# A conditioned transformer block on one core: first LayerNorm as (x - mean) * rs on GpSimd, and a new order for the first 260 tasks

## The chip, the cores and the metric

The kernel runs on one core of a Trainium2 chip. The metric is device time in microseconds (us). Engines carry their names from the profile: PE (matrix products; PEld is its weight load), ACT (scalar engine), DVE (vector engine), POOL (GpSimd), SP (which here only issues DMA transfers).

## What is computed

One block over 2048 tokens of width 512: a LayerNorm with scale and shift from a conditioning vector, linear attention over 32 heads of 16 with softmax features, a residual, a second LayerNorm of the same kind, and a gated feed-forward of width 1376. All inputs are bf16.

```python
mod = (_silu(c) @ w_mod).reshape(c.shape[0], 6, 1, -1)      # sa, ca, ga, sb, cb, gb
h = _layernorm(x, axis=-1) * (1 + ca) + sa
x = x + ga * _A_ref(h, A_wqkv, A_w_phi, A_wo)
h = _layernorm(x, axis=-1) * (1 + cb) + sb
x = x + gb * _B_ref(h, B_w_gate, B_w_up, B_w_down)
```

`_A_ref` makes q, k and v from h, multiplies q and k of each head by a 16 x 16 matrix `w_phi`, takes softmax of the result and of its negative as features, sums features times v over all tokens, and divides. The change touches only the first LayerNorm and the order of the work around it.

## The kernel before, in words

The 2048 tokens are 16 tiles of 128 rows. All work is cut into some 1,230 tasks, each a few instructions on one engine with the buffers it needs. A long string, `ORDER` (line 39), lists all tasks by hand. `arrange` (line 137) walks through it: it hands out buffers from small pools (eight PSUM banks, eight xn tiles, and so on, a freed one going to the end of its pool's line) and gives each task to an engine: the first in the task's list of alternatives, or the one that a letter behind `@` names (A is ACT, D is DVE, P is POOL). Each engine then runs its tasks strictly in this order and waits in front of each for what the task reads and for its buffer. So the string sets five queues at once: PE, ACT, DVE, POOL, and SP, which issues all large transfers.

The tasks that the change and the steps below it speak of (t is a tile, g a group of tiles: group 0 is tile 0, group 1 tile 1, group 2 tiles 2 and 3, and so on to group 8 with tiles 14 and 15; j is one of four 128-row blocks of the width):

- `ld_...` loads on SP: x in seven pieces (x0a, x0b, x1a, x1b, x2a, x2b, x3a), the k weights (wk0, wk1), four quarters of the first two vectors of w_mod (wm00a, wm00b, wm01a, wm01b), wv, the ga part of w_mod (wmga), the last three parts (wmm2), wo. `wqT0` to `wqT3` load the q weights transposed by DMA (line 669).
- `warm0`, `warm1_i` (line 600): idle products of 512 columns on PE, whose result nobody reads.
- `tpw`, `wTc` (lines 661, 664): transposes of the k weights on PE, and their copies out of PSUM. `fold1j`, `fold0j`, `foldc` (lines 679, 685): the k and q weights times the block-diagonal w_phi (`bd`, line 580, built on POOL), and their copies.
- `st1_t` (lines 702, 703): mean and variance of a tile on DVE. `rs1_g` (lines 709 and 710 on ACT, 712 and 713 on POOL): 1/sqrt(variance + eps). `nmr1_g` (line 718): -mean*rs for each tile of a group, on DVE. `xn1_t`: the normalized tile; tile 0 on DVE as (x - mean) * rs (line 729), tile 1 on ACT as x*rs + nmr (line 727), all others on POOL as x*rs + nmr (line 731).
- `tphgj` (line 744): transposes of the normalized group on PE; for groups 6 and 7 the DMA does it (`xT1_t`, line 736). `hm1_gj` (lines 751, 753): scale and shift by the conditioning, out of PSUM, on ACT or DVE (groups 6 and 7 also on POOL).
- `modc1.0`, `modc1.1` (line 630): the conditioning's products for the first LayerNorm, in two halves, out of columns of w_mod; `modc1c0`, `modc1c1` copy them. hm1 of blocks j = 0, 1 needs the first half, j = 2, 3 the second. `modca`, `modc2` (line 616): the rest of the conditioning.
- `Kt` (some in halves a and b, line 817), `Vt` (line 821), `Qt` (line 871): products of a tile with the folded k weights, the v weights, the folded q weights. `et`, `qet` (line 776): exponentials on ACT. `nt`, `qnt` (line 780): sums on DVE. `rt` (lines 794 and 795 on ACT, 798 on DVE): reciprocals. `phit`, `qphit`: features. `vat` (line 836): copy of v. `kvt` (line 282): features times v. `pTt` (line 874): transposes of q features by DMA.

What follows (attention output, second LayerNorm, feed-forward with tasks g, tg, u, hm, y) is the larger part of the string.

Of the kernel before, what the change touches and what calls it, by code (L numbers as in the profile page):

```python
# [51 lines left out]
phi6.0 hm1_73@P n9.0 r9.0@A kv5.0 gwa gra gwb e11.4 e14.0 K10 phi7.0@D kv6.0 K12 V10 kv7.0 e14.4 r8.0 n11.6 n11.2 r11.6 phi9.0 e10.0 e12.0 ld_wd ld_wu0 grb  # L52
n11.4 n14.0 r11.2 n14.4 r14.0 n10.0 r14.4@A phi8.0 va8 V11 V14 n12.0 e11.0 K13 n11.0 phi11.6 r11.4 wo1 r11.0 va10 r10.0@A va11 kv8.0 kv9.0 phi11.2@D phi11.0@D
phi10.0@D phi11.4@D V12 K15 e13.0 wmod_free ld_wg0 phi14.4 phi14.0 kv10.0 kv11.4 kv11.6 Q6 kv11.0 e13.4 r12.0@A e15.4 n13.0 n13.4 r13.0 r13.4 n15.4 e15.0 va14
V15 V13 qe6.0 va12 kv11.2 n15.0 r15.0 r15.4@A va13 phi13.4 Q5 phi15.4 phi13.0@D va15 phi15.0@D phi12.0@D wo0 wo3 Q3 kv12.0 kv13.0 kv14.0 kv15.0 qn6.0 kvn0 kvz0
kv13.4 kv14.4 kv15.4 kvz1 kvn1 num0a num1a num2a wo2 rd0a wo_all rd1a qe3.0 u0a num0b num4a num1b rd0b Q11 qe5.0 rd2a u0b u2a rd4a num2b qn3.0 u1a rd1b tpo0 Q8
qphi6.0@P qphi6.1@P oT0 out0 num4b rd2b u1b wd0 qe11.0 u2b qphi3.1@P qphi3.0@P x1_0 rd4b st2_0 qe8.0 Q7 qe7.0 tpo1 oT1 Q10 Q9 out1 Q15 oT2 rs2_0 qn5.0 nmr2_0
xn2_0 u4a u4b x1_1 qn7.0 tsw xnT0 out2 qphi5.1@P qphi5.0@P pT6 mod02 mod00 qphi7.0@P pT3 mod03@A mod01@A qe15.0 qphi7.1@P Q13 g0.8 x1_2 tg0.8 g0.1 st2_1 wd1
rs2_1 tg0.1 u0.8 u0.1 g0.0 num3b g0.4 hm0.1 hm0.8 pT5 qe9.0 tg0.4 g0.9 wd2 u0.4 u0.9 rd3b u3b tg0.9 g0.5 num3a hm0.4 hm0.9 u0.2 u0.0 num6a tg0.5 tg0.0 rd3a u3a
u0.5 g0.2 hm0.0 hm0.5 rd6a nmr2_1 qe10.0 tg0.2 oT4 g0.10 u0.10 wd6 hm0.2 g0.3 pT7 tg0.3 u6a g0.6 num6b u0.3 y0.0 y0.1 rd6b tg0.10 hm0.10 hm0.3 num5a num5b u6b  # L60
rd5b wd3 wd4 wd5 oT3 oT6 xn2_1 qe13.0 tg0.6 rd5a y0.2 u5b g0.7 tg0.7 out4 u5a oT5 qn11.0 u0.6 u0.7 xnT1 num7a hm0.6 hm0.7 mod13@A mod12@A rd7a x1_4 y0.3 out3
qphi11.1@P qphi11.0@P x1_3 st2_3 out6 mod10@A mod11@A g1.2 tg1.2 g1.1 tg1.1 num7b wd7 u1.3 u1.2 hm1.2 u7a g1.4 u1.1 y0.4 rd7b hm1.1 u1.4 y0.5 tg1.4 hm1.4 g1.0
g1.10 u1.10 g1.3 u7b st2_2 rs2_2 tg1.10 tg1.3 hm1.10 hm1.3 pT11 out5 tg1.0 u1.7 g1.7 x1_6 nmr2_2 u1.0 hm1.0 g1.5 u1.5 x1_5 qn10.0 wd8 y0.6 g1.6 oT7 xn2_2 xn2_3
g1.8 y0.7 Q14 y0.8 wd10 tg1.7 tg1.5 hm1.5 out7 u1.8 u1.6 st2_4 tg1.6 xnT2 xnT3 wd9 x1_7 qphi10.0 Q12 hm1.7 st2_6 mod21@P mod20@P qphi10.1@P y1.0 pT10 tg1.8
mod22@A mod23@A hm1.6 g1.9 y1.1 y1.2 tg1.9 u1.9 y0.9 y1.3 y1.4 g2.5 y0.10 g2.6 st2_5 qe12.0 st2_7 hm1.8 qn9.0 tg2.5 qe14.0 rs2_4 hm1.9 rs2_3 nmr2_4 y1.5 u2.0
g2.1 g2.0 tg2.0 xn2_7@D hm2.0 nmr2_3 fin0 y1.6 g2.2 tg2.2 u2.6 u2.2 hm2.2 u2.1 num11b y1.7 g2.4 rd11b u11b xn2_6@P xnT7 xnT6 u2.5 tg2.1 xn2_5 qphi9.1@P hm2.1
tg2.6 u2.8 xn2_4 hm2.5 g2.3 num11a rd11a u11a u2.9 qphi9.0@P xnT5 y1.8 xnT4 tg2.4 u2.4 hm2.4 hm2.6 tg2.3 g2.9 u2.3 hm2.3 g2.8 tg2.8 tg2.9 u2.7 mod41@P mod43@P
# [991 lines left out]
```

## Time and profile before

| what | value |
|---|---|
| median of 3 runs | 203.72 us (203.69 to 203.81) |
| the profiled execution | 205.47 us |
| its span in the profile | 203.7 us |
| PE busy | 197.0 us, 97% of the span |
| DVE busy | 160.6 us, 79% |
| ACT busy | 106.1 us, 52% |
| POOL busy | 102.8 us, 50% |
| mean granted PE clock | 0.992 |

The span is the time from the first to the last instruction that the profile shows; the execution's own time is 1.77 us longer. In rows of the time-ordered view the first number is the start, the second the time from start to end of the row (`x5` means five instructions merged into one row), and brackets give idle time of the engine before it and what ended it. Because instructions are pipelined, the price of one is better read from its start to the start of the next. Shares over the whole span say little here, since the first 70 us and the rest have different limits.

### The profile page before, as it was taken

The page shows a single profiled execution, that of the slowest core. Times are in us where ns is not written, and L with a number is a line of the kernel's source. Part 1 is how long each engine was busy: PE and PEld are TensorE (multiplying, and loading weights), DVE is VectorE, ACT ScalarE, POOL GpSimd, SP SyncE. Part 2 cuts the span into 40 slices and gives each one's busy share as a digit, 9 for nine tenths or more (in the row PEclk, how much of TensorE's full clock was granted, in tenths as well). Part 3 has the DMA queues.
Part 4 walks back from the last instruction along what each step waited for, and adds up shares of the span by engine and source line. Part 5 has one row for each costly group of instructions (what it writes and reads, how often), then busy time and mean ns, then how long its engine had stood idle before and what let it go on. Part 6 is the DMA issues. An engine that isn't in the chain of part 4 may idle for free.

```text
span 203.7 us, 4159 instructions
## 1 busy us (share of the span) xinstructions
PE 197.0 (97%) x1471; PEld 107.0 (53%) x1471; DVE 160.6 (79%) x375; ACT 106.1 (52%) x252; POOL 102.8 (50%) x144
## 2 busy tenths in 40 slices
...
GB/s 163 328 255 263 275 223 70 136 74 196 392 330 26 147 117 55 77 53 97 118 59 119 36 69 103 80 103 77 26 26 58 23 79 27 31 27 5 53 53 55
DMA packets 49453, 22.94 MB, mean 113 GB/s; under 512 B 38065, under 2 KB 47634, under 8 KB 49426
## 3 DMA queue, kind: packets, MB, share of 16 engines
...
HBM read 11.58 MB, written 2.10 MB: 67 GB/s over the span
## 4 chain that ended last, share of the span: by engine, by line
PE 79%; DMA 8%; ACT 5%; SPq 3%; DVE 3%; issue 1%
PE y_ps L485 19%; PE u_ps L447 18%; PE g_ps L447 17%; PE k_ps L817 6%; PE a_ps L356 6%; DMA wg_sb<-in_B_w_gate_dram 5%; PE v_ps L821 4%; DMA wmod_sb<-in_w_mod_dram 3%; PE q_ps L871 3%; ACT e L776 2%; PE num L326 2%; SPq L537 1%; PE g_ps L449 1%; PE tp_h L744 1%; PE kvacc L282 1%
## 5 line engine op out<-in xcount | busy, mean ns | idle before, releaser
L457 ACT ACTIVATE tg<-g_ps 128x512 bf16<-128x512 f32 (+5 forms) x66 | 28.8, 455 | 67.0 <-PE g_ps L447 39.4
L485 PE MATMUL y_ps<-wd_sb,wmod_sb 128*128 128x512 bf16 (+4 forms) x187 | 45.7, 366 | 0.0
L468 DVE SCALAR_TENSOR_TENSOR wmod_sb<-tg,u_ps 128x512 bf16<-128x512 bf16 (+4 forms) x63 | 30.2, 491 | 18.2 <-ACT tg L457 11.6
L447 PEld LDWEIGHTS <-wg_sb 128*128 128x128 bf16 (+1 forms) x252 | 21.9, 99 | 16.1
L447 PEld LDWEIGHTS <-wu_sb 128*128 128x128 bf16 (+1 forms) x252 | 21.9, 99 | 16.0 <-issue 0.3
L784 POOL TENSOR_TENSOR qphi<-qe,qks 128x512 bf16<-128x512 bf16 x24 | 25.1, 1060 | 3.9 <-DMA pT<-qphi 1.2
L485 PEld LDWEIGHTS <-wmod_sb 128*128 128x128 bf16 (+1 forms) x187 | 17.1, 98 | 16.0 <-issue 0.6
L447 PE MATMUL u_ps<-wT_sb,wu_sb 128*128 128x512 bf16 (+2 forms) x124 | 23.8, 322 | 0.0
L447 PE MATMUL g_ps<-wT_sb,wg_sb 128*128 128x512 bf16 (+2 forms) x124 | 23.1, 322 | 0.0
L447 PE MATMUL g_ps<-wqk_sb,wg_sb 128*128 128x128 bf16 (+4 forms) x128 | 20.0, 287 | 0.0
L447 PE MATMUL u_ps<-wqk_sb,wu_sb 128*128 128x128 bf16 (+4 forms) x128 | 19.8, 287 | 0.1
L780 DVE TENSOR_REDUCE ks<-e 128x64 f32<-128x1024 bf16 (+2 forms) x22 | 19.1, 904 | 0.4 <-ACT e L776 0.4
L780 DVE TENSOR_REDUCE qks<-qe 128x64 bf16<-128x1024 bf16 x16 | 19.2, 1204 | 0.0
L492 DVE TENSOR_TENSOR ot<-y_ps,x 128x512 bf16<-128x512 f32 (+2 forms) x17 | 11.0, 653 | 10.3 <-PE y_ps L485 10.2
L376 POOL TENSOR_SCALAR ve<-mv 128x2 f32<-128x2 f32 (+1 forms) x8 | 1.8, 221 | 33.8 <-DVE mv L366 33.7
L776 ACT ACTIVATE e<-k_ps 128x512 bf16<-128x512 f32 (+2 forms) x44 | 18.0, 515 | 0.0
L817 PE MATMUL k_ps<-wqk_f,h1T 128*128 128x512 bf16 x64 | 17.9, 402 | 0.0
L776 ACT ACTIVATE qe<-q_ps 128x512 bf16<-128x512 f32 x32 | 17.4, 618 | 0.6 <-POOL phi L787 0.4
L356 PE MATMUL a_ps<-wo_sb,oT 128*128 128x512 bf16 x64 | 16.3, 379 | 0.0
L787 POOL TENSOR_TENSOR phi<-e,kr 128x1024 bf16<-128x1024 bf16 (+2 forms) x10 | 14.4, 1449 | 3.6 <-ACT kr L795 2.1
L821 PE MATMUL v_ps<-wv_sb,h1T 128*128 128x512 bf16 x64 | 16.1, 379 | 0.0
L871 PE MATMUL q_ps<-wqk_f,h1T 128*128 128x512 bf16 x64 | 15.9, 379 | 0.0
...
## 6 DMA issues: line engine op xcount, KB each, us to landing
...
wu_sb<-in_B_w_up_dram SPq DMA_DIRECT2D x1, 1376.0 KB, 11.0
wg_sb<-in_B_w_gate_dram SPq DMA_DIRECT2D x1, 1376.0 KB, 10.4
...
```

What stands on the lines that cost most here:

```text
L356: pe.matmul(ap_[:], lhsT=oT[:, j, :], rhs=wo_sb[:, j, :], start=(j == 0), stop=(j == KT - 1))
L447: pe.matmul(ps[:fsz, 0:n], lhsT=w[:, j, ft * P:ft * P + fsz], rhs=h[:, j, 0:n], start=(j == 0), stop=(j == KT - 1))
L457: G.add(f"tg{k}.{ft}", {"ACT": 0.13 + n * 0.00083}, lambda e, tg=tg, g_ps=g_ps, fsz=fsz, n=n: act.activation(tg[:fsz, 0:n], g_ps[:fsz, 0:n ...
L468: dve.scalar_tensor_tensor(hm_all[:fsz, hm[k].slot, ft, 0:n], tg[:fsz, 0:n], 1.0, u_ps[:fsz, 0:n], op0=ALU.add, op1=ALU.mult)
L485: mm = pe.matmul(y[:, 0:c1 - c0], lhsT=hm_all[:fsz, hm[k].slot, ft, tl * P:(tl + 1) * P], rhs=wd_sb[:fsz, ft, c0:c1], start=(ft == 0), sto ...
L776: act.activation(ee[:, a:b, s].rearrange("p g f h -> p g (f h)"), kp[:, a * 64:b * 64].rearrange("p (g n) -> p g n", n=64), ACT.Exp, scale ...
L780: dve.tensor_reduce(ks[:, a:b].rearrange("p g s h -> p (g s) h"), ee[:, a:b].rearrange("p g s f h -> p (g s) h f"), axis=AX.X, op=ALU.add)
L784: engine(e).tensor_tensor(ph[:].rearrange("p (g s f h) -> p g s f h", s=2, f=DH, h=4)[:, :, s], ee[:, :, s], ks[:, :, 1 - s].unsqueeze(2). ...
L787: engine(e).tensor_tensor(ph[:, a * P:b * P].rearrange("p (g f h) -> p g f h", f=DH, h=4), ee[:, a:b].rearrange("p g s f h -> p (g s) f h" ...
L817: pe.matmul(kp[:], lhsT=h1T[:, j, t * P:(t + 1) * P], rhs=wqk_f[:, j, D:2 * D], start=(j == 0), stop=(j == KT - 1))
L821: pe.matmul(vp[:], lhsT=h1T[:, j, t * P:(t + 1) * P], rhs=wv_sb[:, j, :], start=(j == 0), stop=(j == KT - 1))
L871: pe.matmul(qp[:], lhsT=h1T[:, j, t * P:(t + 1) * P], rhs=wqk_f[:, j, 0:D], start=(j == 0), stop=(j == KT - 1))
```

## The change

Three things, and nothing else in the program:

1. xn1 of tiles 2 to 15 on POOL computes (x - mean) * rs, with the mean and rs as the two per-row operands, instead of x*rs + nmr. The nmr1 tasks of groups 2 to 8 are gone (seven tasks, 14 DVE instructions). Only tile 1, on ACT, keeps its one nmr1 product.
2. There are 14 idle products `warm1_i` instead of 12.
3. The first tasks of the string, all those ahead of `pT1`, stand in a new order: 274 before, 269 after. From `pT1 pT4 ld_wd2 tph81` on the string is unchanged, word for word. Some tasks change their engine: rs1_0 and rs1_6 from ACT to POOL, rs1_4 from POOL to ACT, wTc1 from ACT to DVE, r1.0 from DVE to ACT, hm1_00, hm1_42 and hm1_52 from DVE to ACT, hm1_13, hm1_20, hm1_41, hm1_43 and hm1_50 from ACT to DVE. In SP's queue wk1 goes ahead of wk0, x0b ahead of everything but x0a as before, wm00b ahead of x1a, wm01a ahead of wm01b; x3a and wv go ahead of wqT1, the four wqT stand in a row, wmga goes behind them and behind xT1_11 and xT1_10, and wo behind pT2.

The diff, with the string cut at the first lines of each version:

```diff
-wdz pmem warm0 ld_x0a st1_1 rs1_1 st1_0 c1 c2 ld_x0b warm1_0 warm1_1 warm1_2 warm1_3 ld_wk0 ld_wk1 nmr1_1 xn1_1@A st1_3 warm1_4 st1_2 rs1_0 xn1_0 tph11 tpw1
-tpw0 ld_x1b ld_x1a wTc1 warm1_5 tpw2 ld_wm00b c3 tph10 tph03 tph00 st1_7 tpw3 bd rs1_2@P tph13 wTc0 nmr1_2 xn1_3 xn1_2 warm1_6 ld_wm00a st1_6 wTc2 st1_4 st1_5
-wTc3 fold11 fold10 warm1_7 foldc11 ld_x2b fold13 warm1_8 st1_11 foldc10 fold12 warm1_9 foldc13 modc1.0 warm1_10 ld_wm01b tph20 foldc12 warm1_11 rs1_4@P nmr1_4
-ld_wm01a modc1c0 hm1_11@A hm1_10@A tph02 rs1_3@P tph01 tph23 hm1_20@A hm1_01@A st1_10 tph21 hm1_21@A hm1_00 modc1.1 modc1c1@D rs1_6 nmr1_3 tph22 tph12 ld_x2a
-wqT1 hm1_22 hm1_13@A hm1_03 xn1_7 K1a K0a hm1_02@A hm1_23@A xn1_6 tph42 tph40 xn1_5 hm1_40@A st1_8 tph41 ld_x3a xn1_4 K3a hm1_42 hm1_12@A ld_wv0 nmr1_6 tph43
-K3b hm1_41@A xn1_11 tph30 xn1_10 st1_9 rs1_5@P hm1_30@A tph31 wqT3 tph32 K1b ld_wmga st1_15 st1_14 hm1_31@A fold01 foldc01 K0b tph33 wqT2 rs1_8@P K2a K2b hm1_33
-nmr1_5 V0a wqT0 V0b V3a xn1_9 e3.0 V1a xT1_11 e0.0 fold03 n3.0 V1b nmr1_8 xn1_14 va0 e2.0 n0.0 st1_13 r0.0 modca.0 modca.1 xn1_15 st1_12 xn1_8 foldc03 n2.0
-modcac e1.0 hm1_32@A V2a fold02 phi0.0 n1.0 r1.0 fold00 V2b foldc02 foldc00 r3.0 va1 xT1_10 hm1_60@P ld_wmm2 va2 r2.0@A hm1_62@P tph82 hm1_82@A tph50 phi2.0@D
-phi1.0@D hm1_50@A hm1_63@P V3b K4a K4b rs1_7@P Q0 Q2 kv0.0 Q1 qe0.0 va3 qe2.0 hm1_43@A qe1.0 modc2.0 tph52 modc2.1 tph51 nmr1_7 xn1_12 xn1_13 phi3.0@D ld_wo
-qn0.0 modc2c e4.0 kv1.0 qn2.0 hm1_52 kv2.0 Q4 K5a kv3.0 xT1_12 xT1_13 qphi0.0@P qphi0.1@P qn1.0 qe4.0 qphi2.1 tph80 K5b hm1_80@A hm1_51@A e5.0 pT0 qphi2.0 n4.0
-r4.0@A qn4.0 n5.0 phi4.0@D qphi1.1@P hm1_61@P qphi1.0@P tph53 V5 K7a V4 va5 hm1_53@A V6 pT2 hm1_70@P qphi4.1 va4 hm1_71 mask4 va6 K6a K7b K6b e6.0 K8 tph83
-hm1_83 r5.0 qphi4.0@P e8.0 pT1 pT4 ld_wd2 tph81 hm1_81 n6.0 n8.0 e7.0 n7.0 V7 kv4.0 hm1_72@P K11 K9 V9 K14 V8 r6.0@A e9.0 va7 va9 r7.0@A e11.2 e11.6 phi5.0
...
+wdz pmem bd warm0 ld_x0a ld_x0b st1_1 c1 warm1_0 rs1_1 warm1_1 st1_0 rs1_0@P warm1_2 c2 nmr1_1 st1_2 st1_3 c3 xn1_1 warm1_3 warm1_4 warm1_5 warm1_6 ld_wk1 tpw2
+wTc2 rs1_2@P xn1_3 tpw3 xn1_2 xn1_0 tph10 ld_wk0 tpw1 tpw0 wTc3 wTc0 fold12 fold13 wTc1@D fold11 fold10 foldc12 foldc11 foldc10 warm1_7 warm1_8 tph20 warm1_9
+tph00 tph13 ld_x1b st1_6 st1_7 rs1_4 xn1_6 ld_wm00b ld_x1a st1_4 warm1_10 ld_wm00a xn1_7 st1_5 rs1_3@P xn1_4 foldc13 ld_x2b st1_11 modc1.0 tph01 warm1_11
+warm1_12 modc1c0 hm1_00@A hm1_10@A ld_wm01a tph23 tph21 tph11 hm1_20 tph40 tph22 warm1_13 tph41 hm1_21@A hm1_01@A hm1_40@A ld_wm01b st1_10 modc1.1 hm1_41 K3a
+hm1_11@A tph03 modc1c1@D hm1_13 hm1_23@A tph42 hm1_22 tph12 tph02 hm1_42@A hm1_12@A K0a K2a hm1_02@A xn1_5 hm1_03 ld_x2a st1_9 tph31 tph30 hm1_30@A hm1_31@A K3b
+tph32 hm1_32@A tph33 tph43 rs1_6@P xn1_11 xn1_10 st1_8 hm1_43 ld_x3a st1_14 st1_15 e3.0 K2b e2.0 hm1_33 ld_wv0 st1_13 rs1_5@P xn1_9 K0b e0.0 V1a V2a V1b rs1_8@P
+xn1_14 xn1_15 V3a V3b va3 K1a va1 wqT1 K1b fold01 V0a wqT3 wqT2 foldc01 fold02 e1.0 wqT0 fold03 n3.0 fold00 foldc00 V2b n0.0 n2.0 r0.0 xT1_11 foldc03 foldc02
+xT1_10 hm1_60@P hm1_63@P r2.0@A V0b V6 va0 n1.0 r1.0@A tph80 K4a K4b xn1_8 tph50 hm1_50 va2 ld_wmga modca.0 phi0.0 Q0 qe0.0 modca.1 modcac hm1_80@A st1_12
+rs1_7@P phi1.0@D Q1 qe1.0 kv0.0 phi2.0@D kv1.0 Q2 qe2.0 kv2.0 K6a tph53 hm1_53@A hm1_62@P r3.0 phi3.0@D Q4 e4.0 qe4.0 V5 va5 xn1_13 ld_wmm2 xT1_13 K5a kv3.0
+xn1_12 xT1_12 qn0.0 qphi0.0@P qphi0.1@P pT0 qn1.0 K5b K6b qn2.0 qphi2.0 qphi2.1 pT2 n4.0 tph51 e5.0 n5.0 tph52 hm1_52@A modc2.0 modc2.1 va6 r4.0@A hm1_51@A K7a
+tph82 hm1_82@A V4 va4 modc2c qn4.0 phi4.0@D K7b qphi1.0@P hm1_61@P qphi1.1@P hm1_71 e6.0 K8 qphi4.1 tph83 mask4 hm1_83 r5.0 hm1_70@P qphi4.0@P e8.0 ld_wo pT1
+pT4 ld_wd2 tph81 hm1_81 n6.0 n8.0 e7.0 n7.0 V7 kv4.0 hm1_72@P K11 K9 V9 K14 V8 r6.0@A e9.0 va7 va9 r7.0@A e11.2 e11.6 phi5.0 phi6.0 hm1_73@P n9.0 r9.0@A kv5.0
...
@@ -600,7 +599,7 @@
                 pe.matmul(ps[:], lhsT=wd_sb[:, FT - 1, 0:P], rhs=wd_sb[:, FT - 1, :], start=True, stop=True)
         G.add(nm, {"PE": dur}, f, bufs=[ps], **kw)
     warm("warm0", 6, 2.4, r=["wdz"], w=["warm"])
-    for i in range(12):
+    for i in range(14):
         warm(f"warm1_{i}", 1, 0.22, r=["c1"], w=["warm"])
 
     def modc_task(nm, chs, rks, wk, f2, dur):
@@ -712,7 +711,7 @@
                 pool.tensor_scalar(ve1[:, sl], mv1[:, sl, 1], 1e-5, None, op0=ALU.add)
                 pool.tensor_tensor(rs1[:, sl], ve1[:, sl], mhalf[:, sl], op=ALU.pow)
         G.add(f"rs1_{g}", {"ACT": 0.43, "POOL": 1.1}, f_rs, r=[("mv1", t) for t in ts], w=[("rs1", g)])
-        if g:
+        if g == 1:
             def f_nm(e, ts=ts):
                 for t in ts:
                     dve.tensor_scalar(nmr[:, 0, t:t + 1], mv1[:, t, 0:1], rs1[:, t:t + 1], -1.0, op0=ALU.mult, op1=ALU.mult)
@@ -725,11 +724,9 @@
             def f_xn(e, t=t, xn=xn):
                 if e == "ACT":
                     act.activation(xn[:], x_sb[:, t, :], ACT.Identity, scale=rs1[:, t:t + 1], bias=nmr[:, 0, t:t + 1])
-                elif e == "DVE":
-                    dve.tensor_scalar(xn[:], x_sb[:, t, :], mv1[:, t, 0:1], rs1[:, t:t + 1], op0=ALU.subtract, op1=ALU.mult)
                 else:
-                    pool.tensor_scalar(xn[:], x_sb[:, t, :], rs1[:, t:t + 1], nmr[:, 0, t:t + 1], op0=ALU.mult, op1=ALU.add)
-            G.add(f"xn1_{t}", {"POOL": 0.69, "ACT": 0.73} if t else {"DVE": 0.3}, f_xn, r=[("rs1", g)] + ([("nmr1", g)] if t else []), w=[("xn1", t)],
+                    engine(e).tensor_scalar(xn[:], x_sb[:, t, :], mv1[:, t, 0:1], rs1[:, t:t + 1], op0=ALU.subtract, op1=ALU.mult)
+            G.add(f"xn1_{t}", {"ACT": 0.73} if t == 1 else {"POOL": 0.69} if t else {"DVE": 0.3}, f_xn, r=[("rs1", g)] + ([("nmr1", g)] if t == 1 else []), w=[("xn1", t)],
                   bufs=[xn], port=("POOL", "DVE"))
         if TD[g]:
             for q, t in enumerate(ts):
```

More of the change, by code (lines that the diff above doesn't have):

```diff
@@ L52 @@
[L52 to L67, printed above, removed]
```

53 lines of the change are left out of this document (34 added, 19 removed).

## The prediction

> **What bounds the kernel now.** I read the page first for the span, then busy time by stretches, then each engine in order of time over the first 45 us, then the waits there, and last the transfers. The profiled execution took 205.47 us: the span and 1.77 us around it. The median without profile is 203.72 us, 1.75 us less, so I work out a difference on the trace and take it from the median.
>
> ```profile
> span 203.7 us, 4159 instructions
> ```
> ```profile
> 4.02:7.43 3.41, 2.32 (x20) 1.08 (x19) 3.27 (x11) 2.08 (x7) 1.71 (x3) 1.00 1.04 325
> 10.85:14.26 3.41, 2.92 (x48) 1.85 (x47) 3.23 (x14) 3.12 (x11) 3.24 (x7) 1.00 1.26 218
> 14.26:17.67 3.41, 3.41 (x16) 1.76 (x15) 3.13 (x10) 2.54 (x7) 2.60 (x5) 0.50 1.15 345
> 11.80:40.87 29.07, 28.50 (x267) 16.25 (x267) 27.35 (x60) 27.59 (x66) 24.20 (x34) 0.94 0.87 197
> 13.44:40.25 26.81, 26.62 (x255) 15.22 (x253) 25.16 (x53) 25.33 (x61) 22.02 (x29) 0.94 0.84 203
> 41.00:58.00 17.00, 17.00 (x138) 8.72 (x136) 16.86 (x34) 16.58 (x54) 13.63 (x11) 1.00 0.87 245
> 70.00:200.10 130.10, 129.97 (x875) 70.30 (x873) 95.69 (x225) 44.35 (x97) 45.97 (x64) 1.00 0.33 64
> ```
>
> The columns behind the stretch's length are PE, PEld, DVE, ACT, POOL, granted clock, DMA share, GB/s. From 70 us to the end PE never rests, and from 41 to 58 us PE, DVE and ACT are all full. So the part of the order that the change leaves alone runs as one solid block, and what decides is how early the new first part hands over to it. I set the fourth and fifth stretch so that they end with that part's last task on ACT (e8, 40.87 us) and on DVE (r5, 40.25 us); on PE the part ends with V7. All three engines must come earlier if the block is to come earlier: the smallest of the three shifts is the gain.
>
> In 11.80 to 40.87 us ACT is idle for 29.07 - 27.59 = 1.48 us, and in 13.44 to 40.25 us DVE for 1.65 us. Most of that has one cause:
>
> ```profile
> ACT h1T L751 <- PE tp_h L744: 1.3, 2, 0.7
> DVE h1T L753 <- PE tp_h L744: 0.9, 2, 0.6
> ```
>
> Both wait for PE's transposes, at 15 to 20 us, and PE is late there because its clock is granted at 0.50 for just one stretch, 14.26 to 17.67 us: 3.41 us at half speed lose 1.71 us of products. Why does the clock fall there? PE in the stretch two before it (kept its clock) and in the one just before the fall:
>
> ```profile
> 4.11 1.25 PE L600 MATMUL warm<-wd_sb 128*128 128x512 bf16 x5
> 6.41 0.23 PE L744 MATMUL tp_h<-ident,xn 128*128 128x128 bf16 x1 [1.05 <-POOL bd L580]
> 6.68 0.62 PE L661 MATMUL tp_w<-ident,wqk_sb 128*128 128x128 bf16 x8
> 7.13 0.38 PE L600 MATMUL warm<-wd_sb 128*128 128x512 bf16 x1
> ```
> ```profile
> 11.36 0.38 PE L600 MATMUL warm<-wd_sb 128*128 128x512 bf16 x1
> 11.79 0.27 PE L744 MATMUL tp_h<-ident,xn 128*128 128x128 bf16 x2
> 11.90 0.38 PE L600 MATMUL warm<-wd_sb 128*128 128x512 bf16 x1
> 12.34 0.60 PE L744 MATMUL tp_h<-ident,xn 128*128 128x128 bf16 x6
> 13.26 0.55 PE L630 MATMUL modc_ps<-sc_bf,wmod_sb 128*128 128x1 bf16 x16 [0.32 <-DMA wmod_sb<-in_w_mod_dram]
> 13.67 0.47 PE L744 MATMUL tp_h<-ident,xn 128*128 128x128 bf16 x3
> 13.98 0.77 PE L817 MATMUL k_ps<-wqk_f,h1T 128*128 128x512 bf16 x2
> ```
>
> Busy time does not explain it: 2.92 us before the fall, only 2.32 us where the clock stayed. Columns streamed do: 5 x 512 + 128 + 8 x 128 + 512 = 4224 where it stayed; 2 x 512 + 11 x 128 + at most 2 x 512 = 3456 before the fall (the modc products stream one column each). So I take it that somewhere between 3456 and 4224 columns in 3.41 us the clock is kept.
>
> **The change, part by part.** *PE and its clock.* The start stays where it is: modc1.1 waits for the last quarter of w_mod, which is as before behind ten earlier loads of the same sizes, so it starts near 13.26 us (the row with the DMA wait). Ahead of it the new order puts three idle products (warm1_11 to 13) and twelve transposes into the deciding stretch, and behind it K3a and three transposes by 14.26 us: 3 x 512 + 12 x 128 + 2 x 512 + 3 x 128 = 4480 columns, above the 4224 that kept the clock. I forecast that the half-clock stretch goes. The two added products themselves stand ahead of modc1.1 or in the wait for the first weights; they cost nothing while PE has to wait for that load anyway, and at about 0.22 us each (five took 1.25 us with their tail) 0.44 us if that cover is gone. Behind modc1.1, PE's work to V7 is the old one less about four transposes (0.2 us). PE's term: 1.71 + 0.2 = 1.9 us.
>
> The Trainium skill, "TensorE: Matmul & The Clock Gate", Part 1, says that a free-running window of about 3.4 us sets the clock and that it falls after an idle window. The length agrees with 3.41 us; the idle window does not, for PE was busy 2.92 us of the one before the fall.
>
> *ACT.* Rows of its prices, each to the start of the next:
>
> ```profile
> 11.80 2.07 ACT L751 ACTIVATE h1T<-tp_h,modc 128x128 bf16<-128x128 bf16 x5
> 13.74 0.31 ACT L709 ACTIVATE ve<-mv,eps 128x2 f32<-128x2 f32 x1
> 14.08 0.20 ACT L710 ACTIVATE rs<-ve 128x2 f32<-128x2 f32 x1
> 14.19 1.24 ACT L751 ACTIVATE h1T<-tp_h,modc 128x128 bf16<-128x128 bf16 x3
> ```
> ```profile
> 24.34 0.68 ACT L751 ACTIVATE h1T<-tp_h,modc 128x256 bf16<-128x256 bf16 x1
> 24.79 1.20 ACT L685 CAST wqk_f<-fold_ps 128x512 bf16<-128x512 f32 x2
> ```
> ```profile
> 26.68 0.43 ACT L794 ACTIVATE ks<-ks 128x64 f32<-128x64 f32 x1
> 27.21 0.26 ACT L795 ACTIVATE kr<-ks 128x64 bf16<-128x64 f32 x1
> 27.37 1.00 ACT L751 ACTIVATE h1T<-tp_h,modc 128x256 bf16<-128x256 bf16 x2
> ```
>
> An hm1 of one tile is 1.94/5 = 0.39 us, of two 0.45, an rs1 0.45, an r 0.69. Behind 11.80 us ACT loses hm1_20, 41, 43, 50 (1.80), hm1_13 (0.39) and rs1_6 (0.45) and gains hm1_00 (0.39), hm1_42, 52 (0.90) and r1.0 (0.69): 0.66 us less. With PE on time its 1.33 us of waiting goes, and 0.15 us stays: 11.80 + 27.59 - 0.66 + 0.15 = 38.88 against 40.87. ACT's term: 2.0 us. I looked where ACT could wait anew: the fold copies, e, va and qe each find their product finished earlier when PE runs at full clock, so none is late next.
>
> *DVE.*
>
> ```profile
> 21.78 0.33 DVE L718 TENSOR_SCALAR nmr<-mv,rs 128x1 f32<-128x1 f32 x2
> 22.02 1.21 DVE L780 TENSOR_REDUCE ks<-e 128x64 f32<-128x1024 bf16 x1
> ```
> ```profile
> L753 DVE TENSOR_SCALAR h1T<-tp_h,modc 128x256 bf16<-128x256 bf16 (+1 forms) x8 | 2.9, 375 | 0.9 <-PE tp_h L744 0.9
> L798 DVE RECIPROCAL kr<-ks 128x64 bf16<-128x64 f32 x4 | 2.0, 528 | 0.0
> ```
>
> A pair of -mean*rs costs 0.24 us; seven pairs go, five of them behind 13.44 us: 1.20. Five hm1 come and three go (2 x 0.375 = +0.75), r1.0 goes (-0.53): 0.98 us less. Its 0.9 us of waits for transposes goes, 0.75 stays: 13.44 + 25.16 - 0.98 + 0.75 = 38.37 against 40.25. DVE's term: 1.9 us. wTc1 on DVE has no row; a half-size read from PSUM is the 0.375, so 0.4 to 0.75 us, and it stands ahead of DVE's wait for the next rows of x, which hides it; without that cover it costs ACT's next fold copy as much.
>
> *POOL.* (x - mean) * rs has the same shape as the old form; no row shows it on POOL, so I bound it by the shortest and the longest of the old ones,
>
> ```profile
> L731 POOL TENSOR_SCALAR xn<-x_sb,rs,nmr x14: 762/767/1182, 9.5 to 31.2; 128x512 bf16<-128x512 bf16 x14
> ```
>
> 0.76 and 1.18 us, and take the median, 0.77; one subtraction in place of an addition gives no reason for less. POOL no longer waits for DVE's products, takes rs1_0 and rs1_6 and gives up rs1_4 (about 1 us more in all). On a walk with these prices the sixth xn1 is ready near 14.7 us and its transposes are due near 15.4; at 1.18 us each that cover is gone and about 1 us of the gain with it.
>
> *SP.* The first transposed load of the q weights (wqT1) moves behind x3 and wv, so that all four now stand in a row; w_mod's ga part moves behind the last two of them and two transposes of xn1 (so it now waits for POOL's xn1_11 and xn1_10), wo behind pT2, and pT1 now queues behind wo. Users: the q folds, due near 21 us; modca, due near 24 us; wo, due after 50 us. I cost these at nothing; the rival below is that this fails.
>
> **Sum.** PE 1.9, ACT 2.0, DVE 1.9: the block starts 1.9 us earlier, and everything behind it with it. 205.47 - 1.9 = 203.57 profiled, **201.8 us** for the median of 203.72. With DVE's remaining idle gone and PE's short stops too, at most 2.4; with xn1 at its dear end, 1.0.
>
> **Rivals.** *The clock doesn't change.* Either 4480 columns don't hold it, or the stretch's edges lie elsewhere against the work, or the runs without a profile never had the fall (the 1.75 us by which they are shorter is close to the 1.71 us). In the first cases PE stays the bound and gains its 0.2 us and its few short stops (28.50 us busy of 29.07); in the last ACT has 0.66 us less to do and DVE 0.98. All give about 0.7 us, 0.2 to 1.1: 203.0. For it: thin margin in columns. Against it: the three runs lie within 0.12 us, which a wandering fall would spread. By the skill's idle window the two idle products would not matter, since no window was idle, which is this rival.
>
> *Slower: the q weights come late.*
>
> ```profile
> 10.89 0.57 SPq L537 DMA_DIRECT2D x_sb<-in_A_x_dram  x1
> 11.52 0.50 SPq L551 DMA_DIRECT2D wv_sb<-in_A_wqkv_dram  x1
> 12.06 1.62 SPq L669 DMA_TRANSPOSE wT_sb<-in_A_wqkv_dram  x1
> ```
> ```profile
> x_sb<-in_A_x_dram SPq DMA_DIRECT2D x1, 512.0 KB, 5.1
> ```
> ```profile
> wT_sb<-in_A_wqkv_dram SPq DMA_TRANSPOSE x1, 7.4
> ```
>
> x3 lands at 10.89 + 5.1 = 16.0 us, the transposed load behind it and wv at 12.06 + 7.4 = 19.5: of these 3.5 us wv's 512 KB take about 1.6, so one transposed load may take 1.9. Four in a row behind wv (near 17.1 us) end at 24.7 at that price. PE reaches fold00 near 21.4 us (13.7 + 14 half K and V of two products, 6.2, + 27 transposes and folds at 0.45/8, 1.5), and V2b, V0b, V6, K4, Q0 queue behind it: 3.3 us of waiting against 1.9 gained, 205.1 us. It decides from a landing near 23.7 us on. Against it: SP issues x3, wv and the four in a row from about 9.3 us (10.89 less one transposed load of 1.6), so the fourth is issued near 9.3 + 0.57 + 0.50 + 3 x 1.62 = 15.2 us, and even at the 7.4 us that include a queue of 1 MB it lands at 22.6.
>
> *The gain is given back* between 41 and 70 us by something tied to a fixed time: no load there is, all hang on SP's order, so little chance; 203.7.
>
> **Numbers.** Less than 0.2% (0.41 us) a measurement of this kernel can't tell from no change. Forecast 0.50 (201.4 to 202.7), clock rival 0.27 (202.6 to 203.5, 0.03 of it within 0.2%), given back 0.09, slower 0.14. Faster 0.74, same 0.12, slower 0.14. The range goes from 2.4 us gained to 0.2, 201.3 to 203.5, and leaves out the slower rival and part of the same.
>
> **What would show it.** Granted clock 1.00 from 14 to 18 us; V7 on PE 1.9 us earlier, e8's end on ACT near 38.9, r5's on DVE near 38.4; no wait of ACT or DVE for tp_h over 0.3 us; no PE wait at the q folds. Wrong if the 0.50 stretch stands, if it appears at another place with PE due, or if V7 comes early and 70 us does not.

## The result and the profile after

The changed kernel takes 223.03 us (median, 222.92 to 223.61) against 203.76 us for the kernel before: 1.094 times as long, 95% interval 1.089 to 1.098. The prediction of 201.8 us was wrong, and its sign too.

The first view is the changed kernel's page: the span, then the chain that ended last, by engine and by line.

```profile
span 221.9 us, 4119 instructions
...
PE 59%; POOL 17%; DVE 9%; ACT 5%; DMA 4%; issue 3%; SPq 0%; POOLq 0%; ACTq 0%; DVEq 0%
PE y_ps L484 17%; PE u_ps L446 16%; PE g_ps L446 16%; POOL xn L728 12%; PE a_ps L355 5%; ACT e L773 3%; DMA pT<-qphi 3%; DVE ks L777 2%; PE num L325 2%; POOL rs L712 2%; DVE st L701 1%; DMA x_sb<-in_A_x_dram 1%; PE g_ps L448 1%; PE q_ps L868 1%; POOL qphi L781 1%
```

One line of POOL now carries 12% of the chain, 27 us. It is the changed normalization (line 731 before, 728 now). Its own view gives shortest, median and longest in ns, and who waited for it:

```profile
L728 POOL TENSOR_SCALAR xn<-x_sb,mv,rs x14: 2069/2074/2087, 8.6 to 45.7; 128x512 bf16<-128x512 bf16 x14
...
  PEld L741: 13.3, 6
  PE tp_h L741: 10.4, 6
```

One instruction takes 2.07 us where it took 0.77. The longest is within 1% of the shortest, which speaks against contention with a neighbour; the forms below settle it. The transposes wait for it, and what waits for the transposes follows. The stretches (the columns are those of the prediction) and the first stop on PE, in order of time:

```profile
10.00:20.00 10.00, 6.34 (x60) 4.14 (x62) 5.11 (x16) 4.74 (x14) 9.81 (x8) 0.59 0.86 222
20.00:30.00 10.00, 9.70 (x60) 4.71 (x58) 8.19 (x16) 8.65 (x19) 9.63 (x8) 0.89 0.16 27
30.00:40.00 10.00, 3.54 (x19) 1.38 (x19) 2.10 (x4) 2.53 (x8) 9.81 (x9) 0.62 0.56 210
```
```profile
9.13 0.59 PE L599 MATMUL warm<-wd_sb 128*128 128x512 bf16 x2
12.76 0.39 PE L741 MATMUL tp_h<-ident,xn 128*128 128x128 bf16 x2 [3.04 <-POOL xn L728]
...
18.02 0.61 PE L629 MATMUL modc_ps<-sc_bf,wmod_sb 128*128 128x1 bf16 x16
```

From 10 to 40 us POOL is the only engine that is full in all three stretches (9.81, 9.63, 9.81 of 10); PE is full in the second alone (9.70). modc1.1, forecast near 13.26 us, comes at 18.02, since PE takes its tasks in order and the transposes of the second pair stand ahead of it. The clock falls on top: 0.59, 0.89 and 0.62 in these stretches. It falls for the first time within the 3.04 us stop, near 11.9 us, when PE has been idle for 2.2 us. The Trainium skill ("TensorE: Matmul & The Clock Gate", Part 1) says that the clock falls after an idle window of some 3.4 us; the trace does not agree, for PE was busy for 1.25 of the 3.41 us ahead of the fall. What the lower clock adds to the loss is not told apart here; around 35 us it can't be much, since PE has work for 3.54 us of ten.

V7 shows how late the unchanged block begins (the prediction let the reordered part end with it; in the string it is the second task on PE behind that part). In order of time, the changed kernel:

```profile
56.28 1.03 PE L818 MATMUL v_ps<-wv_sb,h1T 128*128 128x512 bf16 x4
```

In the profile of before it stood at 39.13 us (its row is shown further down), 17.15 us earlier; the two profiled executions differ by 223.61 - 205.47 = 18.1 us. The last microsecond comes at the very end, and is taken up below.

### The profile page after: what moved, and what is told of

It is laid out like the page before. It is cut to its first block, busy times and chain, and to the rows that moved or that the text cites. A ratio compares the mean times of both kernels' runs of the same rounds, so it can differ in the third digit from the quotient of the medians.

```text
span 221.9 us, 4119 instructions
## 1 busy us (share of the span) xinstructions
PE 201.9 (91%) x1450; PEld 109.0 (49%) x1473; DVE 161.2 (73%) x363; ACT 105.9 (48%) x249; POOL 122.9 (55%) x146
## 4 chain that ended last, share of the span: by engine, by line
PE 59%; POOL 17%; DVE 9%; ACT 5%; DMA 4%; issue 3%; SPq 0%; POOLq 0%; ACTq 0%; DVEq 0%
PE y_ps L484 17%; PE u_ps L446 16%; PE g_ps L446 16%; POOL xn L728 12%; PE a_ps L355 5%; ACT e L773 3%; DMA pT<-qphi 3%; DVE ks L777 2%; PE num L325 2%; POOL rs L712 2%; DVE st L701 1%; DMA x_sb<-in_A_x_dram 1%; PE g_ps L448 1%; PE q_ps L868 1%; POOL qphi L781 1%
## 5 line engine op out<-in xcount | busy, mean ns | idle before, releaser
L484 PE MATMUL y_ps<-wd_sb,wmod_sb 128*128 128x512 bf16 (+4 forms) x180 | 44.2, 366 | 0.2
L467 DVE SCALAR_TENSOR_TENSOR wmod_sb<-tg,u_ps 128x512 bf16<-128x512 bf16 (+4 forms) x63 | 30.2, 491 | 18.1 <-ACT tg L456 11.6
L728 POOL TENSOR_SCALAR xn<-x_sb,mv,rs 128x512 bf16<-128x512 bf16 x14 | 29.0, 2076 | 0.5
L814 PE MATMUL k_ps<-wqk_f,h1T 128*128 128x512 bf16 x61 | 19.4, 440 | 1.4 <-ACT e L773 1.3
L868 PE MATMUL q_ps<-wqk_f,h1T 128*128 128x512 bf16 x61 | 17.4, 406 | 0.2
L741 PE MATMUL tp_h<-ident,xn 128*128 128x128 bf16 x48 | 7.4, 271 | 10.7 <-POOL xn L728 10.4
```

Of the source, the lines that this page charges most:

```text
L467: dve.scalar_tensor_tensor(hm_all[:fsz, hm[k].slot, ft, 0:n], tg[:fsz, 0:n], 1.0, u_ps[:fsz, 0:n], op0=ALU.add, op1=ALU.mult)
L484: mm = pe.matmul(y[:, 0:c1 - c0], lhsT=hm_all[:fsz, hm[k].slot, ft, tl * P:(tl + 1) * P], rhs=wd_sb[:fsz, ft, c0:c1], start=(ft == 0), sto ...
L728: engine(e).tensor_scalar(xn[:], x_sb[:, t, :], mv1[:, t, 0:1], rs1[:, t:t + 1], op0=ALU.subtract, op1=ALU.mult)
L814: pe.matmul(kp[:], lhsT=h1T[:, j, t * P:(t + 1) * P], rhs=wqk_f[:, j, D:2 * D], start=(j == 0), stop=(j == KT - 1))
L868: pe.matmul(qp[:], lhsT=h1T[:, j, t * P:(t + 1) * P], rhs=wqk_f[:, j, 0:D], start=(j == 0), stop=(j == KT - 1))
```

## The experiments

The theory after the result: the form on POOL is the whole loss (14 x 1.3 us, all on the path), and order and idle products do what the prediction said. The rival: the new order loses by itself, whatever a normalization costs. Both turned out to be partly right. Times are medians; the kernel before, timed again beside each group of runs, stood at 203.8 to 204.0 us.

### One part of the change alone

**order_only**: the new order and the 14 idle products, with the old x*rs + nmr and the nmr1 tasks put back by hand ahead of their users, for which six xn1 tasks and one rs1 stand at other places in the string. Tile 1's normalization falls to POOL in it; **order_old_form** puts it back on ACT.

```diff
-                    engine(e).tensor_scalar(xn[:], x_sb[:, t, :], mv1[:, t, 0:1], rs1[:, t:t + 1], op0=ALU.subtract, op1=ALU.mult)
+                    pool.tensor_scalar(xn[:], x_sb[:, t, :], rs1[:, t:t + 1], nmr[:, 0, t:t + 1], op0=ALU.mult, op1=ALU.add)
```

> The new order with its two more idle products, but xn1 on POOL again as x*rs + nmr, with the seven nmr1 tasks put back where DVE passes when rs1 is ready. Theory A (the form is slow: 14 instructions of 2.07 us in place of 0.77): POOL's xn1 rows return to 0.77 us, PE's waits for POOL xn (10.4 us after the change) shrink below 1 us, and the time is near or below the kernel before, 201.8 to 203.8 us. Theory B (the order is at fault: late q weights, POOL's tasks queued badly, and the long xn1 rows only show contention with DVE): the time stays above 214 us.

> The run order_only again with one slip mended: tile 1's xn1 had fallen to POOL there, ahead of everything, and is back on ACT. New order, x*rs + nmr on POOL, nmr1 tasks put in by hand. Theory A1 (with the form at 0.77 us the order is worth what the prediction said): 201.8 to 203.5 us. Theory A2 (the order is worth nothing once POOL and DVE hand -mean*rs back and forth again): POOL waits for nmr about 3 us as in order_only (3.2 us) and the time is 204 to 206 us.

Measured: 208.12 us (ratio 1.019, 1.015 to 1.023) and 206.53 us (1.013, 1.012 to 1.015), both above every range expected for theory A. So the new order with the old form costs 2.7 us; it does not gain. This is not yet the order alone: POOL waits 3.2 us for the products that were put back (nmr), between 4 and 60 us of order_old_form.

**form_only**: the old order and 12 idle products, with (x - mean)*rs on POOL and the nmr1 tasks of groups 2 to 8 gone.

> The old order and 12 idle products, but xn1 of tiles 2 to 15 on POOL as (x - mean) * rs, without the seven nmr1 tasks. Theory A: xn1 rows at 2.07 us, 14 x 1.30 = 18.2 us more on POOL of which it had a few us idle, so 214 to 222 us. Theory B: xn1 rows stay near 0.8 us and the time within 2 us of the kernel before.

Measured: 220.67 us (ratio 1.080, 1.076 to 1.085), 16.7 us above the 204.0 beside it. The form alone is most of the 19.3 us.

### What the form costs

**forms**: the kernel before with eleven forms of the instruction behind POOL's last task, three times each. The kernel's time is of no interest.

```diff
+    def form_sub_mult():
+        pool.tensor_scalar(pr[:], xa, m1, r1, op0=ALU.subtract, op1=ALU.mult)
...
+    def form_add_mult():
+        pool.tensor_scalar(pr[:], xa, n1, r1, op0=ALU.add, op1=ALU.mult)
...
+            form()
```

> The kernel before, and behind its last POOL task eleven forms of one tensor_scalar on POOL, three times each, on 128x512 bf16 (two of them on 128x128), whose results nobody reads. Theory A: subtract then mult with two per-row operands takes 2.07 us also there, where POOL does nothing else, against 0.77 for mult then add; which of the others are slow tells whether it is the operation subtract, the pair of operations, or the mean lying with a stride of two (then the contiguous operand is fast). Theory B: all forms take about 0.77 us there, and the 2.07 us come from DVE running beside POOL.

Groups by line; the last number ahead of the second bar is the mean in ns. From the top: multiply-subtract, subtract-multiply with the mean, the same with a contiguous operand, the same by constants, add alone, multiply alone, subtract alone; subtract-multiply over 128 columns, multiply-add, add-multiply; multiply-add over 128 columns:

```profile
L897 POOL TENSOR_SCALAR probe<-x_sb,rs,nmr 128x512 bf16<-128x512 bf16 x3 | 6.2, 2079 | 0.3
L888 POOL TENSOR_SCALAR probe<-x_sb,mv,rs 128x512 bf16<-128x512 bf16 x3 | 6.2, 2078 | 0.3
L891 POOL TENSOR_SCALAR probe<-x_sb,nmr,rs 128x512 bf16<-128x512 bf16 x3 | 6.2, 2076 | 0.3
L909 POOL TENSOR_SCALAR probe<-x_sb 128x512 bf16<-128x512 bf16 x3 | 5.8, 1926 | 0.3
L903 POOL TENSOR_SCALAR probe<-x_sb,nmr 128x512 bf16<-128x512 bf16 x3 | 4.7, 1574 | 0.3
L906 POOL TENSOR_SCALAR probe<-x_sb,rs 128x512 bf16<-128x512 bf16 x3 | 4.7, 1564 | 0.3
L900 POOL TENSOR_SCALAR probe<-x_sb,mv 128x512 bf16<-128x512 bf16 x3 | 4.7, 1564 | 0.3
...
L915 POOL TENSOR_SCALAR probe<-x_sb,mv,rs 128x128 bf16<-128x128 bf16 x3 | 2.4, 795 | 0.3
L885 POOL TENSOR_SCALAR probe<-x_sb,rs,nmr 128x512 bf16<-128x512 bf16 x3 | 2.3, 772 | 1.2 <-DVE flag L525 1.0
L894 POOL TENSOR_SCALAR probe<-x_sb,nmr,rs 128x512 bf16<-128x512 bf16 x3 | 2.3, 771 | 0.3
...
L912 POOL TENSOR_SCALAR probe<-x_sb,rs,nmr 128x128 bf16<-128x128 bf16 x3 | 1.3, 447 | 0.3
```

The quick and the dear forms alternate there (starts at 169.5 us for multiply-add, 172.1 for subtract-multiply, 185.2 for add-multiply, 187.8 for multiply-subtract), beside the same last products of PE and operations of DVE, which end before 200 us; the short pair (447 and 795 ns) ran behind that, with POOL alone. So the price is the form's own: not the place of the operand (2078 and 2076) and not a neighbour. Two pairs of operations are quick, multiply-add and add-multiply; a subtraction in either place makes the same shape 2.7 times as long, and even one operation alone (1.56 us) is dearer than a quick pair. Among the forms tried there is no other quick one. The Trainium skill ("Trainium Architecture — The Big Picture", The software stack) says that many operations, on POOL above all, go to software handlers, and that some have a surprising latency for that reason. That would fit two prices for one shape, but no run here looks inside.

### The order with a quick form

(x + (-mean))*rs is quick, but something has to make -mean. **order_add_form** has DVE do it, per tile behind its statistics; **order_add_form_12** leaves out the two added idle products as well; **old_order_add_form** is the same form in the old order.

```diff
                 dve.bn_aggr(mv1[:, t, :], st1[:, t, :])
+                if t > 1:
+                    dve.tensor_scalar(nmr[:, 0, t:t + 1], mv1[:, t, 0:1], -1.0, None, op0=ALU.mult)
...
+                        pool.tensor_scalar(xn[:], x_sb[:, t, :], nmr[:, 0, t:t + 1], rs1[:, t:t + 1], op0=ALU.add, op1=ALU.mult)
```

> The changed kernel as it is, but xn1 on POOL as (x + (-mean)) * rs, with -mean made by one small DVE instruction behind each tile's statistics (14 of about 0.11 us, so DVE's part of the gain goes, but POOL waits for no product). The forms run showed add then mult at 0.77 us and subtract then mult at 2.08. Theory A: xn1 rows back at 0.77 us and the whole loss gone: 202.0 to 203.5 us; granted clock 1.00 from 14 to 18 us. Theory B (a part of the loss is the order's): it stays over 205 us, with PE waits that name something else than POOL's xn.

> The same with the two added idle products taken out again. If they hold the clock: the granted clock falls to 0.50 for 3.4 us in the profile or in more of the runs, and the time rises by up to 1.7 us. If they do nothing: the same time and clocks as with them, within 0.3 us.

> The old order and 12 idle products with (x + (-mean)) * rs on POOL and without the seven nmr1 tasks. If the form alone is neutral when it runs at 0.77 us: within 0.5 us of the kernel before, a little below, since POOL no longer waits for nmr (1.4 us there). It splits order_add_form's gain into the form's part and the order's.

Measured: 207.73 (ratio 1.019, 1.017 to 1.021), 208.41 (1.022, 1.020 to 1.023) and 205.87 us (1.009, 1.008 to 1.011). For the first, theory B came true; the third lies 2.1 us above the kernel before, and not within 0.5 as expected (four of its six runs had a clock of 0.992, the two at 1.000 took 204.65 and 204.99 us). The two idle products seem to help: without them the mean clock was 0.990 to 0.992 in all five runs, with them 0.998 or more in three of five. They are not enough to hold it: order_add_pair_wo below has them too, and five of its nine runs had 0.992. The 0.7 us between the medians lie at the edge of what the two intervals can tell apart.

**order_free** asks for the order by itself: POOL adds the mean instead of subtracting it, the quick form with nothing to negate. So the computation is changed in its sign only, and the change is as cheap as the prediction took it to be.

> The changed kernel with GpSimd's first normalization as (x + mean)*rs, the form that took 0.77 us there: it adds the mean instead of subtracting it, so that no operation for -mean or -mean*rs is needed anywhere, and everything else is as the change has it. This is the change as the prediction costed it. If the prediction's sum was right but for the 1.3 us per normalization: 201.3 to 203.0 us. If the new order loses by itself, because its walk of the first 60 us was too hopeful: above 204.5 us, with the first wait on PE near 13 to 15 us and a second loss between 40 and 58 us as in the two kernels with the fast form (206.5 and 207.7).

Measured: 205.69 us (ratio 1.008, 1.005 to 1.011). The form is therefore 223.03 - 205.69 = 17.3 us, and 1.8 us of loss are left that have nothing to do with it. It also prices -mean on DVE: 207.73 - 205.69 = 2.0 us, and some 0.9 us more, since order_free lost that much at the last store, which order_add_form did not (see the section on DVE's program): about 2.9. DVE in order of time, in order_add_form and then in order_free:

```profile
11.76 0.69 DVE L701 BATCH_NORM_STATS2 st<-x_sb 128x6 f32<-128x512 bf16 x1
12.48 0.18 DVE L702 BATCH_NORM_AGGREGATE mv<-st 128x2 f32<-128x6 f32 x1
12.69 0.15 DVE L704 TENSOR_SCALAR nmr<-mv 128x1 f32<-128x1 f32 x1
12.76 0.68 DVE L701 BATCH_NORM_STATS2 st<-x_sb 128x6 f32<-128x512 bf16 x1
...
13.79 0.41 DVE L755 TENSOR_SCALAR h1T<-tp_h,modc 128x256 bf16<-128x256 bf16 x1
```
```profile
11.47 0.66 DVE L701 BATCH_NORM_STATS2 st<-x_sb 128x6 f32<-128x512 bf16 x1
12.16 0.18 DVE L702 BATCH_NORM_AGGREGATE mv<-st 128x2 f32<-128x6 f32 x1
12.26 0.40 DVE L753 TENSOR_SCALAR h1T<-tp_h,modc 128x256 bf16<-128x256 bf16 x1
```

A 0.15 us instruction adds 0.2 us start to start (1.00 us from a tile's statistics to what follows them, where it was 0.79). Adding up tile by tile, this starts the scale-and-shift hm1_20 at 13.79 us and not at 12.26; PE stands behind it, because the PSUM bank that it empties is the one that the next idle product takes. order_add_form's PE:

```profile
14.25 0.58 PE L599 MATMUL warm<-wd_sb 128*128 128x512 bf16 x1 [1.02 <-DVE h1T L755]
```

### The load in front of the transposes

order_free starts well: V7 stands at 36.83 us. What it then loses shows in its waits between 40 and 60 us:

```profile
ACT e L776 <- DMA pT<-qphi: 1.4, 1, 1.4
```

In the new order the output projection's 512 KB (ld_wo) are requested ahead of pT1 and pT4; ACT's e6 needs a buffer that such a transpose frees. **order_free_wo** moves that request back ahead of pT0 to pT4, and nothing else:

```diff
-... ld_wmm2 xT1_13 ... qphi4.0@P e8.0 ld_wo pT1 pT4
+... ld_wmm2 ld_wo xT1_13 ... qphi4.0@P e8.0 pT1 pT4
```

> As order_free (the mean is added, not subtracted), with one load moved back: the output projection's weights are requested before the transposes pT0 to pT4, as in the old order, not between pT2 and pT1. In the kernel with -mean on DVE, ACT's e6 waited 1.39 us for a transpose pT near 45 us. If that load in front of pT1 is what is lost between 40 and 58 us: 0.8 to 1.5 us less than order_free. If the transposes wait for something else, or PE for another engine there: within 0.4 us of order_free.

Measured: 204.28 us (ratio 1.001, 0.999 to 1.003), 1.41 us less, and the wait of ACT for pT is gone from its waits. The one load is 1.4 us.

### What the shorter program of DVE costs

order_free_wo should now lead. It does until PE's last products, which begin at 189.53 us, against 190.61 in **before_nmr_pair** below, and yet both spans end at 202.6 and 202.7 us. The last DVE operation and the transfers around the end, of order_free_wo (time-ordered view, then the view of transfers from 198.0 us on):

```profile
198.02 0.91 DVE L492 TENSOR_TENSOR ot<-y_ps,x 128x512 bf16<-128x512 f32 x2 [1.39 <-PE y_ps L485]
```
```profile
q14 instruction: 1, 0.01, 0.8%
...
out_dram<-ot SPq DMA_DIRECT2D x1, 32.0 KB, 2.5
```

From DVE's last end (198.93) to the span's end are 3.7 us; in the kernel before it was 2.65. The last store takes 2.5 us to land instead of 1.5, and a packet of instructions (queue q14, one of 8 KB) lies in the same two microseconds. So it is in the profiles of five kernels (after, form_only, order_free, order_free_wo, old_order_free; 2.3 to 2.5 us), all those in which DVE's program lost the 14 products and nothing was put in for them. In all the others the last store lands in 1.5 us, also in order_add_pair_wo, where 14 went and 7 came and the packet lies about 1 us ahead of the store's request. **order_free_wo_pad** puts 14 idle memsets in, at 1.2 us, where DVE waits for x; **after_pad** does it in the changed kernel, **old_order_free_pad** in **old_order_free** (old order, 12 idle products, the mean added).

```diff
+    def f_pad(e):
+        for _ in range(14):
+            dve.memset(nmr[:, 0, 2:3], 0.0)
+    G.add("pad", {"DVE": 1.0}, f_pad, w=["pad"])
```

> order_free_wo (the mean is added, not subtracted) with 14 idle memsets of one column on DVE at about 1.2 us, where DVE waits 2.5 us for x. They restore the length of DVE's program and should cost nothing there. If the length of DVE's program sets whether an instruction packet lies beside the last store: the last store lands in 1.5 us instead of 2.5, the span ends 2.7 us after DVE's last operation instead of 3.7, and the time is 203.2 to 203.5 us instead of 204.28. If the late landing has another cause: 204.1 to 204.5.

> The changed kernel as it is, with the same 14 idle memsets on DVE. By the program's length: about 222.1 us, 0.9 less than the changed kernel's 223.03. By another cause: 222.9 to 223.6.

> The old order with 12 idle products, GpSimd's normalization as (x + mean)*rs (adds the mean, not subtracts), and the seven tasks that made -mean*rs gone. It shows what leaving out 14 small DVE operations is worth by itself. If DVE's 2.9 us of them lay on the path: 201.5 to 203.0 us. If another wait ended last at each place (rs, the transposes): 203.3 to 204.0, no difference.

> old_order_free (204.80 us; the mean is added, not subtracted) with the same 14 idle memsets on DVE. By the program's length: 203.7 to 204.0, so that leaving out the small products gives nothing and the 0.95 us that it lost were the last store. By another cause: 204.6 to 205.0.

Measured: order_free_wo_pad 203.39 us (ratio 0.996, 0.994 to 0.999), after_pad 222.30, 0.7 less than the changed kernel. The same views of order_free_wo_pad (span 201.5 us), where no q14 packet is left in the last 3.6 us:

```profile
197.93 0.91 DVE L492 TENSOR_TENSOR ot<-y_ps,x 128x512 bf16<-128x512 f32 x2 [1.39 <-PE y_ps L485]
```
```profile
q1 hardware_dynamic: 297, 0.17, 15.9%
...
out_dram<-ot SPq DMA_DIRECT2D x1, 32.0 KB, 1.5
```

Fourteen instructions more make the kernel 0.9 us shorter. In all four padded kernels (order_add_pool_wo_pad below is the fourth) the last store lands in 1.5 us. For the pair in the old order the time doesn't follow, and both expectations of a time were missed: 204.80 without and 205.07 us with the memsets, whose runs scattered from 203.75 to 206.40. Its profile shows where 1 us went: SP took 4.30 us over two transposes of xn1 (3.15 in the kernel before), the load behind them came later, and PE waited 1.03 us for it at 29.13 us, a wait that the profiles of before and forms don't have. So in the old order only the landing confirms the theory. That the packet itself holds up the store is not shown, only that the two come and go together; why was not found out.

### Is there a version that beats both?

**before_nmr_pair** makes the two products of a group with one DVE instruction, in the kernel before. **order_add_pair_wo** is the new order with the load moved back, the quick form, and -mean of a group by one DVE instruction. **order_add_pool_wo_pad** has POOL make it, and the memsets besides. None of them leaves anything out.

```diff
+                dve.scalar_tensor_tensor(nmr[:, 0, sl], mv1[:, sl, 0], -1.0, rs1[:, sl], op0=ALU.mult, op1=ALU.mult)
...
+            G.add(f"nm1_{g}", {"DVE": 0.1}, lambda e, sl=sl: dve.tensor_scalar(nmr[:, 0, sl], mv1[:, sl, 0], -1.0, None, op0=ALU.mult),
...
+            G.add(f"nm1_{g}", {"POOL": 0.3}, lambda e, sl=sl: pool.tensor_scalar(nmr[:, 0, sl], mv1[:, sl, 0], -1.0, None, op0=ALU.mult),
```

> The kernel before with one change: the two products -mean*rs of a group are made by one DVE instruction over two columns instead of two instructions of 0.20 us. Nothing is left out. Seven DVE instructions fewer, some 1.4 us of DVE between 5 and 30 us. If DVE's small operations hold GpSimd's normalizations back there: 202.5 to 203.4 us. If they do not end last: 203.5 to 204.0, no difference.

> A version that leaves nothing out: the new order, GpSimd's normalization as (x + (-mean))*rs, -mean of a group's two tiles by one DVE operation behind the later of their statistics, and the output projection's load moved back before the transposes pT. With -mean on DVE per tile the time was 207.73; the load's place took 1.4 of it, and half of the 14 operations are gone. If DVE's operations cost by their number: 204.5 to 205.5. If only the one between 13 and 15 us costs: 203.3 to 204.0. It beats the kernel before only below 203.4.

> Leaves nothing out: the new order, the load moved back, 14 idle memsets on DVE at 1.2 us, GpSimd's normalization as (x + (-mean))*rs, and -mean of a group's two tiles by one GpSimd operation ahead of the group's rs, seven of about 0.3 us start to start (as the additions of eps to the variance, 0.23 us). If DVE's seven operations were what cost 3.0 us over the version that adds the mean: 203.4 to 204.0, and GpSimd's extra 2.1 us lie mostly beside its waits. If every operation ahead of a normalization costs what it takes, on whichever engine: 205 to 205.6.

Measured: 204.08 (ratio 1.001, 0.999 to 1.004), 206.40 (1.011, 1.007 to 1.014) and 204.95 us (1.005, 1.003 to 1.006). None beats the kernel before. Against the 203.39 us of the kernel with nothing to negate, seven small operations cost 3.0 us on DVE (V7 at 39.07 against 36.83 us, and five of nine runs at a clock of 0.992; the four others took 205.5 to 205.9 us, so some 2.4 us are left without the clock) and 1.6 on POOL, where each stands ahead of two normalizations. The expectation that most of POOL's seven would lie beside its waits failed; so did the two ranges for order_add_pair_wo.

## Why the prediction was wrong

**POOL, the step that failed.** "One subtraction in place of an addition gives no reason for less" is the step, with its bound of 0.76 to 1.18 us. Both ends of the bound came from the one row of the old form, so they said how much that form varies, and nothing of another. It measured 2.08. The walk knew that 1.18 us would use up the cover; at 2.08, POOL's 14 normalizations are 29 us of work, where in the row of before the first starts at 9.5 us and the last at 31.2. Of the change's 19.3 us, 17.3 are this, with the lower clock that its waits bring.

**SP, costed at nothing.** Wrong by 1.4 us. The working named the users of the moved load (wo, due after 50 us), and that pT1 queues behind it, but not the user of pT1. The moves of the q weights were right: no wait for a transposed load of the q weights is among order_free's, and the slower rival did not come.

**PE and its clock.** Against the profile the walk was right, once the form is quick: in order_free the clock is 1.00 from 10 to 18 us, modc1.1 starts at 13.26 us as forecast, and V7 stands 2.3 us earlier than in the profile of before (1.9 forecast). But that gain is no gain of the time. The rival had it: the runs without a profile hardly ever had the fall. Of the 33 runs of the kernel before that stand beside order_free, 32 had a mean clock of 0.998 or more and took 203.6 to 204.6 us; the one at 0.992, as in the profile, took 206.35. And time is span plus 1.7 to 1.9 us in the runs of every kernel. So the 1.77 us "around the span" were real, the 1.75 us between profile and median were the fall of the clock, and a difference worked out on that trace must not be taken from that median.

The run forms shows what should have been the base: up to 169 us it is the kernel before, and the clock of the profiled execution didn't fall there. Its stretch from 10 to 18 us, and then three marks of the handover (V7 on PE, the exponentials up to e8 on ACT, r5 on DVE) in before, in forms and in order_free:

```profile
10.00:18.00 8.00, 7.48 (x88) 4.51 (x85) 7.70 (x28) 7.66 (x21) 7.45 (x12) 1.00 1.20 279
```
```profile
39.13 1.02 PE L821 MATMUL v_ps<-wv_sb,h1T 128*128 128x512 bf16 x4
38.95 3.05 ACT L776 ACTIVATE e<-k_ps 128x512 bf16<-128x512 f32 x6
39.79 0.54 DVE L798 RECIPROCAL kr<-ks 128x64 bf16<-128x64 f32 x1
```
```profile
37.77 1.02 PE L821 MATMUL v_ps<-wv_sb,h1T 128*128 128x512 bf16 x4
37.59 3.06 ACT L776 ACTIVATE e<-k_ps 128x512 bf16<-128x512 f32 x6
38.47 0.54 DVE L798 RECIPROCAL kr<-ks 128x64 bf16<-128x64 f32 x1
```
```profile
36.83 1.03 PE L821 MATMUL v_ps<-wv_sb,h1T 128*128 128x512 bf16 x4
36.91 3.04 ACT L776 ACTIVATE e<-k_ps 128x512 bf16<-128x512 f32 x6
37.84 0.55 DVE L798 RECIPROCAL kr<-ks 128x64 bf16<-128x64 f32 x1
```

From before to order_free ACT's mark comes 2.04 and DVE's 1.95 us earlier, where 2.0 and 1.9 were forecast; from forms to order_free PE's comes 0.94, ACT's 0.68 and DVE's 0.63 us earlier, and that is what the order is worth when the clock doesn't fall. The rule of columns (kept somewhere between 3456 and 4224) is not shown: in forms the same products in the same order as before lie some 0.14 us later, PE is busy for 2.94 us from 10.85 to 14.26 us as it was for 2.92 before, and the clock stays. (Whether the stretches begin elsewhere in that execution can't be seen, since its clock doesn't change there.)

**ACT and DVE.** Of their 2.0 and 1.9 us, 1.33 and 0.9 were waits for PE's transposes behind the slow clock, and these went the same way: forms has no such wait. What is left of the sum is seen in order_free_wo_pad, which has all that the forecast assumed: 203.39 us, 0.4 to 0.6 less than before. The clock rival had given 0.7 us, 203.0.

**Given back.** The prediction saw no load that could give the gain back between 41 and 70 us. Two things gave it back: wo ahead of pT1, in that stretch (1.4 us; it hangs on SP's order, where the prediction looked for a fixed time), and the last store, at the end (0.9 us). Of the second no view of before could have told; an edit that takes instructions away had been taken to be free of its own cost.

Put together from below: 203.39, + 0.89 (last store) = 204.28, + 1.41 (load) = 205.69, + 17.34 (form) = 223.03.
